# A fused windowed-attention and Fourier-mixing kernel in fp32: the probabilities of the first two batches turned by small products with the identity into tiles that hold two heads, and the first sines written to tiles that are not yet in use

## The chip, the cores and the metric

The kernel runs on one core of one Trainium2 chip. The metric is the device time in microseconds (us) of one launch; the kernel before took a median of 601.89 us in 3 runs (600.99 to 602.36). A core has five engines that are named here as the profile names them: PE (TensorE, matrix products; PEld is its weight load), DVE (VectorE), ACT (ScalarE), POOL (GpSimd) and SP (SyncE, which issues the loads and stores). Each engine takes its own instructions strictly in the order of the program, and semaphores order them between engines.

## The reference

Eight batches, eight heads, 576 positions, head size 64, with q, k and v in fp32 and the weights in 64-bit floats. Heads 0 to 3 see a window of 32 positions, heads 4 to 7 a window of 32 positions at every fourth one. The attention's result, heads side by side, is the x of a mixing layer of width 512.

```python
scores = np.where(masks, scale * q @ k.T, -1e9)
attn = exp(scores - scores.max(-1)); attn = attn / (attn.sum(-1) + 1e-9)
x = heads_side_by_side(attn @ v)                  # (8, 576, 512)
theta = x @ w_theta
zr, zi = x * np.cos(theta), x * np.sin(theta)
y = einsum('ts,bsd->btd', w_tok_r, zr) + einsum('ts,bsd->btd', w_tok_i, zi)
u = x + y
out = u + np.maximum(u @ w_ch, 0.0)
```

## The kernel before

**Tiling.** Heads go in four pairs. The dilated heads' positions are sorted on the host so that every head sees a plain window, and the 576 queries of a pair fall into 9 blocks of 64, each against its block of 64 keys and the one ahead. x, y, u and the output are held as four tiles of 128 features by 576 positions. Products that need fp32 precision run in three: a number is split into a high part in a shorter format (a cast) and a low part (the rest, a subtraction on POOL or DVE), and high by high, high by low and low by high are summed.

**Stages of a batch.** Names are those of tiles in the profile.
- *Attention, per pair.* 18 score products s (L426) of 64 moving columns; mask and row maximum on DVE (L401, into P and mx); exponentials on ACT (L452, nine of 128x64 a pair, with their sums sm; for batch 0 one, L441); sum and reciprocal on DVE (L455, L456); P times the reciprocal on POOL (L458). P has the queries on its partitions, so it is turned before the next product: into pt, the matrix that holds each block's transposed probabilities. From batch 1 on that is done by `turn` (L462 to L477), 8 stream transposes of 32x288 on DVE a pair (L474). For batch 0 it is `flip` (L494 to L515): 9 transposes a pair on PE against the identity idt (L509) in three groups of three, in three PSUM banks, and 12 copies of 64x96 a pair out of them, four on DVE (L487) and eight on ACT (L490). pt is four tiles of 128x9x64, one a head, so that two pairs alternate; the parts outside the window are zeroed once at the start. Then 18 products with v give o (L561), and ACT copies o to x (L525). From batch 1 on x is split in xh for the theta product (L537 ACT, L541 and L543 on DVE or POOL).
- *Trigonometry, per step of 128 positions* (five steps, in the order 4, 0, 1, 2, 3; step 4 has 64 positions). theta th (L606 for batch 0, L624 to L631 later); x transposed to positions on partitions, xn (L658); K is theta over 2 pi rounded (ACT, L680) and then its remainder (DVE, L682); g is its sine (L688); the absolute value and the cosine are taken in K's place (L637, L639); both are multiplied by xn on DVE (L694 for the sine, L644 for the cosine). `zsplit` (L577) splits each product: the high part zh is cast on DVE for batch 0 (L582) and on ACT later (L585), the low part zl is a subtraction on POOL (L587). The tiles K and g have two buffers each (tags f and g), so that a third step can begin only when the first one's zl is done. The zh and zl tiles have a tag for each of the nine (kt 0 to 3 cosines, 4 to 7 sines, 8 step 4).
- *Mixing.* y (L738): per tile of 128 features and half of the positions 27 products, three for each of the nine z; residual u = x + y on DVE (L716), its cast on ACT (L719) and low part on POOL (L721); then the channel product c (L767), 12 a tile, the final max and sum on DVE (L746), and the store.
- *Weights.* They come as 64-bit floats, and are turned into fp32 on DVE (L324, L334 or L329) and ACT (L326, L332), and split by ACT (L342) and POOL (L344). All of this lies before about 120 us.

**What sets the order.** For batch 0 and the part of batch 1's attention that runs beside it, tasks are generators that name an engine and a cost at each step, and the class `Order` (L56) plays them through: the engine that is free first takes the ready task of lowest rank (table RANK). The order that comes out is fixed in the program for every engine. A task can also wait for a named event (for instance ("P", 1, 2): P of batch 1, pair 2) or take one of several buffers. From batch 1's mixing on, loops set the order (`phase`), with batch n+1's attention inside batch n's products.

```python
        if b == 0:
            yield "DVE", dve2(DM)
            pin(nc.vector.tensor_copy(hi, z))
        else:
            yield "ACT", act(DM)
            pin(nc.scalar.copy(hi, z))
```

Of the kernel before, what the change touches and what calls it, by code (L numbers as in the profile page):

```python
# [34 lines left out]
STS = (4, 0, 1, 2, 3)  # L35
KORD = (0, 4, 1, 5, 2, 6, 3, 7, 8)
# [109 lines left out]
def build(ctx, tc, qT, kT, vw, wth, wtk, wch, masks, ident, outT):  # L146
# [315 lines left out]
    def turn(b, pr):  # L462

        yield None, "pts"
        yield None, ("P", b, pr)
        yield None, ("pv",) + divmod(b * NP + pr - 2, NP)
        P, rp = probs.pop((b, pr))
        o = 2 * (pr % 2)
        pmats[b, pr] = pts[o:o + 2]
        for i, (hh, e, o) in enumerate(strips()):  # L470
            if i % 2 == 0:
                yield "DVE", 940
            k0, p0 = QB * (2 * e + o), QB * (2 * e + hh)
            pin(nc.vector.transpose(pmats[b, pr][hh][k0:k0 + QB, :, QB * e:QB * e + QB],  # L474
                                    P[p0:p0 + QB, :, QB * o:QB * o + QB]))
        give("P", rp)
        signal(("pt", b, pr))  # L477

    def flip_evac(ps, rel, pr, m, key):
        for hh in range(2):  # L480
            for e in range(2):
                p0 = QB * (2 * e + hh)
                dst = pmats[0, pr][hh][BW * e:BW * e + BW, 3 * m:3 * m + 3, QB * e:QB * e + QB]
                src = ps[:, :, p0:p0 + QB]
                if m == 0:
                    yield "DVE", 170
                    pin(nc.vector.tensor_copy(dst, src))  # L487
                else:
                    yield "ACT", 174
                    pin(nc.scalar.copy(dst, src))  # L490
        give(*rel)
        signal(key)

    def flip(pr):  # L494
        yield None, ("P", 0, pr)
        if pr >= 1:
            yield None, ("fl", 0, pr - 1)
        if pr >= 2:
            yield None, ("pv", 0, pr - 2)
        yield None, "pts"  # L500
        o = 2 * (pr % 2)
        pmats[0, pr] = pts[o:o + 2]
        P, _ = probs.pop((0, pr))
        for m in range(3):
            ps, rel = yield from bank("mmt"[m], f"pT{pr}_{m}")
            ps = ps[:BW, :3 * 128].rearrange("p (a b) -> p a b", b=128)
            yield "PE", 330
            for n in range(3):
                pe(nc.tensor.transpose(ps[:, n], P[:, 3 * m + n], idt))  # L509
            go(flip_evac(ps, rel, pr, m, ("fe", pr, m)))  # L510
        signal(("fl", 0, pr))
        for m in range(3):
            yield None, ("fe", pr, m)
        give(f"xh{pr}", 0)
        signal(("pt", 0, pr))  # L515
# [31 lines left out]
    def pv(b, pr):  # L547
# [10 lines left out]
        for j in range(NJ):  # L558
            v = va[:, j] if j < VA else vb[:, j - VA]
            for hh in range(2):  # L560
                pe(nc.tensor.matmul(ps[64 * hh:64 * hh + 64, BW * j:BW * j + BW], v[:, 64 * hh:64 * hh + 64],  # L561
                                    pmats[b, pr][hh][:, j], start=True, stop=True))
# [14 lines left out]
    def zsplit(b, kt, z):  # L577
        hi = hp.tile([128, DM], F32R, tag=f"zh{kt}", name=f"zh{b}_{kt}")
        lo = hp.tile([128, DM], F32R, tag=f"zl{kt}", name=f"zl{b}_{kt}")
        if b == 0:  # L580
            yield "DVE", dve2(DM)
            pin(nc.vector.tensor_copy(hi, z))  # L582
        else:
            yield "ACT", act(DM)
            pin(nc.scalar.copy(hi, z))  # L585
        yield "POOL", pool(DM)
        pin(nc.gpsimd.tensor_tensor(lo, z, hi.bitcast(F32), op=ALU.subtract))  # L587
        zs[b, kt] = (hi, lo)
        signal(("z", b, kt))
# [45 lines left out]
    def cosine(b, st, f, z, kt, key):  # L635
# [10 lines left out]
        if kt is not None:  # L646
            yield None, ("px", b, st)
            give(*rx)
            yield from zsplit(b, kt, z)
# [12 lines left out]
    def trig(b, st):  # L662
# [5 lines left out]
        K = gp.tile([128, DM], I32, tag="f", name=f"K{b}_{st}")[:R]  # L668
        f = K.bitcast(F32)
        gt = gp.tile([128, DM], F32, tag="g", name=f"g{b}_{st}")  # L670
# [18 lines left out]
        if R == 128:  # L689
            go(cosine(b, st, f, f, st, ("cos", b, st)))  # L690
# [5 lines left out]
            yield from zsplit(b, 4 + st, g)  # L696
        else:
# [4 lines left out]
            yield from cosine(b, st, f, g, None, ("cos", b, st))  # L702
            give(*rx)
            yield from zsplit(b, 8, gt)
# [19 lines left out]
    def token(b, d, g):  # L724
# [6 lines left out]
        for kt in KORD:  # L731
# [5 lines left out]
            for l, r in ((zh, wh), (zh, wl), (zl, wh)):  # L737
                pe(nc.tensor.matmul(ps, l[:, cs], r, start=(n == 0), stop=(n == 3 * NK - 1)))  # L738
                n += 1
        go(residual(b, d, g, ps, rel), RANK["evacuate"])  # L740
# [193 lines left out]
```

## Time and profile before

| quantity | value |
|---|---|
| runs | 601.89, 600.99, 602.36 us, median 601.89 |
| profiled execution | 601.59 us, its span 599.8 us (1.8 us lie outside), mean granted clock 0.982 |
| first exponential of batch 1 on ACT | 65.75 us |
| first score product of batch 2, third pair | 147.20 us |

The page gives each engine's busy time and share of the span, and the span in 40 slices of 15 us with a digit for the busy tenths and for the TensorE clock that was granted. Other views of the same trace are used beside it: windows (busy time of each engine in each stretch), waits (an instruction that stood idle, its releaser, and how long), groups (all instructions of a line and shape, busy time, mean ns of one, idle time ahead), a timeline (start, length, instruction, with idle time in brackets), and the chain of work that ended last. A few records can be missing.

### The profile page before, as it was taken

To read this page: it belongs to the slowest core of one execution; us is meant where nothing else is said; L and a number is where in the kernel's file an instruction comes from. 1 tells how busy PE (TensorE), PEld (TensorE's weight loads), DVE (VectorE), ACT (ScalarE), POOL (GpSimd) and SP (SyncE) were. 2 spreads that over 40 slices of the span, in tenths; PEclk is the share of its full clock that TensorE was granted. 3 is DMA by queue.
4 is the path that set the end of the run, shared out by engine and by line. 5 is a ranking of instruction groups with operands and counts; after the bars stand their busy time and mean duration, and the time that the engine had idled before them with its cause. 6 is when DMAs were issued, how large, how long until landed. Compare 5 with 4: busy or idle time off the path is not lost.

```text
span 599.8 us, 14024 instructions
## 1 busy us (share of the span) xinstructions
PE 567.4 (95%) x5428; PEld 513.8 (86%) x5428; DVE 367.2 (61%) x1264; ACT 354.5 (59%) x959; POOL 222.5 (37%) x208
## 2 busy tenths in 40 slices
PE   4897599889999999999999999999999999999997
PEld 4644599779998899988998899988998899989997
DVE  3879898775566567656665657655764656444112
ACT  1796958767553974468564784359555685267010
POOL 2237846435142442316324252225323252315220
PEclk9998699999999999999999999999999999999999
DMA  8973347302541054401741035400642022001102
GB/s 322 396 278 99 121 163 246 136 0 87 196 139 61 1 186 148 149 1 40 240 142 61 0 142 180 151 11 17 228 141 97 1 81 97 2 1 42 37 1 80
DMA packets 26722, 67.82 MB, mean 113 GB/s; under 512 B 2848, under 2 KB 3104, under 8 KB 26656
## 3 DMA queue, kind: packets, MB, share of 16 engines
q1 hardware_dynamic: 26656, 66.92, 32.1%
q8 instruction: 43, 0.70, 0.5%
q14 instruction: 23, 0.19, 0.1%
HBM read 57.48 MB, written 9.44 MB: 112 GB/s over the span
## 4 chain that ended last, share of the span: by engine, by line
PE 42%; DVE 25%; ACT 21%; DMA 5%; issue 3%; POOL 3%; SPq 0%; ACTq 0%; POOLq 0%; DVEq 0%
PE y L738 21%; DVE pt L474 11%; PE c L767 9%; ACT P L452 7%; PE o L561 4%; PE th L624 3%; DVE P L401 3%; PE s L426 3%; ACT zh L585 2%; ACT K L639 2%; DVE K L644 2%; ACT g L688 2%; ACT K L637 2%; POOL P L458 2%; PE th L606 2%
## 5 line engine op out<-in xcount | busy, mean ns | idle before, releaser
L721 POOL TENSOR_TENSOR u<-x,u 128x288 fp32r<-128x288 f32 x64 | 54.2, 847 | 186.9 <-ACT u L719 171.5
L474 DVE STREAM_TRANSPOSE pt<-P 32x288 f32<-32x288 f32 x224 | 105.1, 469 | 23.5 <-POOL P L458 20.4
L767 PE MATMUL c<-u,late_wc 128*128 128x288 f32 x768 | 112.9, 299 | 2.2 <-DVE x L716 1.4
L767 PEld LDWEIGHTS c<-u,late_wc 128*128 128x128 f32 x768 | 107.2, 190 | 6.4 <-DVE x L746 2.0
L719 ACT CAST u<-x 128x288 fp32r<-128x288 f32 x64 | 27.4, 430 | 133.4 <-DVE x L716 133.4
L452 ACT ACTIVATE P<-P,mx 128x64 f32<-128x64 f32 x252 | 84.1, 336 | 17.6 <-DVE mx L446 17.4
L738 PE MATMUL y<-wtkh,zh 128*128 128x288 f32 x288 | 91.3, 317 | 3.0 <-DVE zh L582 3.0
L738 PE MATMUL y<-wtkh,zl 128*128 128x288 f32 x288 | 86.5, 300 | 0.9 <-POOL zl L587 0.9
L738 PE MATMUL y<-wtkl,zh 128*128 128x288 f32 x288 | 86.5, 300 | 0.0
L587 POOL TENSOR_TENSOR zl<-g,zh 128x512 fp32r<-128x512 f32 x40 | 52.1, 1302 | 77.4 <-ACT zh L585 64.4
L624 PE MATMUL th<-wthh,xh 128*128 128x512 f32 x224 | 75.9, 400 | 0.0
L716 DVE TENSOR_TENSOR x<-y,x 128x288 f32<-128x288 f32 x64 | 28.8, 451 | 66.7 <-PE y L738 66.4
L738 PE MATMUL y<-late_wt_b,zh 128*128 128x288 f32 x320 | 68.0, 296 | 0.0
L738 PEld LDWEIGHTS y<-wtkh,zh 128*128 128x128 f32 x288 | 55.6, 193 | 6.6 <-DVE zh L582 3.3
L738 PE MATMUL y<-late_wt_a,zh 128*128 128x288 f32 x256 | 57.1, 304 | 2.0 <-DVE x L716 2.0
L738 PEld LDWEIGHTS y<-wtkh,zl 128*128 128x128 f32 x288 | 55.6, 193 | 1.3 <-POOL zl L587 1.3
L738 PEld LDWEIGHTS y<-wtkl,zh 128*128 128x128 f32 x288 | 55.7, 193 | 0.8 <-POOL wtkl L344 0.5
L587 POOL TENSOR_TENSOR zl<-K,zh 128x512 fp32r<-128x512 f32 x32 | 41.9, 1309 | 36.5 <-ACT zh L585 35.1
L401 DVE CUSTOM_DVE_ANT_0 P<-s,msk 128x64 f32<-128x64 f32 x288 | 45.5, 220 | 15.1 <-PE s L426 8.3
L458 POOL TENSOR_TENSOR P<-P,sm 128x576 f32<-128x576 f32 x32 | 38.2, 1197 | 43.6 <-DVE sm L456 22.2
L738 PEld LDWEIGHTS y<-late_wt_b,zh 128*128 128x128 f32 x320 | 51.3, 188 | 0.5 <-POOL late_wt_b L344 0.2
L624 PEld LDWEIGHTS th<-wthh,xh 128*128 128x128 f32 x224 | 42.1, 188 | 8.1
(98 smaller groups left out, 1104.7 us busy)
## 6 DMA issues: line engine op xcount, KB each, us to landing
q<-in_qT_dram SPq DMA_DIRECT2D x32, 576.0 KB, 4.2
va<-in_vw_dram SPq DMA_DIRECT2D x30, 320.0 KB, 2.9
out_dram<-x SPq DMA_DIRECT2D x32, 288.0 KB, 2.1
k<-in_kT_dram SPq DMA_DIRECT2D x28, 304.0 KB, 4.5
vb<-in_vw_dram SPq DMA_DIRECT2D x29, 256.0 KB, 3.1
st_wtk<-in_wtk_dram SPq DMA_DIRECT2D x8, 576.0 KB, 7.8
st_wth<-in_wth_dram SPq DMA_DIRECT2D x4, 512.0 KB, 8.5
st_wch<-in_wch_dram SPq DMA_DIRECT2D x4, 512.0 KB, 3.7
```

The lines of the kernel that those rows point to most:

```text
L401: pin(nc.vector.tensor_tensor_reduce(out=P[:, n], in0=ps[:, n - g0], in1=msk[:, mask_of(pr, n)], op0=ALU.add, op1=ALU.max, scale=1.0, scal ...
L452: table(nc.scalar.activation(P[:, n], P[:, n], AF.Exp, bias=mx[:, n:n + 1], scale=SCALE, accum_out=sm[:, n:n + 1]))
L458: pin(nc.gpsimd.tensor_tensor(P, P, sm.unsqueeze(2).to_broadcast([128, NJ, BW]), op=ALU.mult))
L474: pin(nc.vector.transpose(pmats[b, pr][hh][k0:k0 + QB, :, QB * e:QB * e + QB], P[p0:p0 + QB, :, QB * o:QB * o + QB]))
L561: pe(nc.tensor.matmul(ps[64 * hh:64 * hh + 64, BW * j:BW * j + BW], v[:, 64 * hh:64 * hh + 64], pmats[b, pr][hh][:, j], start=True, stop=T ...
L587: pin(nc.gpsimd.tensor_tensor(lo, z, hi.bitcast(F32), op=ALU.subtract))
L624: pe(nc.tensor.matmul(pt, l, r, start=(n == 0), stop=(n == 3 * NC - 1)))
L716: pin(nc.vector.tensor_tensor(x[:, ts], ps, x[:, ts], op=ALU.add))
L719: pin(nc.scalar.copy(uh[b, d][:, ts], x[:, ts]))
L721: pin(nc.gpsimd.tensor_tensor(ul[b, d][:, ts], x[:, ts], uh[b, d][:, ts].bitcast(F32), op=ALU.subtract))
L738: pe(nc.tensor.matmul(ps, l[:, cs], r, start=(n == 0), stop=(n == 3 * NK - 1)))
L767: pe(nc.tensor.matmul(ps, l[:, cs], r[:, ts], start=(n == 0), stop=(n == 3 * NC - 1)))
```

## The change

- The tile pt is two tiles of 128x9x2x64, both heads of a pair in one, instead of four; `pv` (L561) and `turn` take their parts from there.
- `flip` takes the batch as an argument and is used for batches 0 and 1; `turn` stays for batches 2 to 7. A pair is turned by 18 products of 64x64 with a 64x64 corner of the identity (L512 of the changed kernel), in two PSUM banks of five and four blocks, and taken out by four copies: the first halves of the two groups by DVE (L487, 64x320 and 64x256 elements), the second halves by ACT (L490).
- The steps 4, 0 and 1 of batch 0's trigonometry have K and g in tiles that the later z of steps 2 and 3 would use (FG0: zl2, zl6, zl3, zl7, zh3, zh7), so only steps 2 and 3 take the two buffers of f and g. The planner takes and gives these buffers by name, and `zsplit` gives them back.
- The cosines' high parts of batch 0 (kt 0 to 3) are cast on ACT, the sines' on DVE as before.
- `zsplit` of batch 1 waits in the planner for the token products of batch 0.

```diff
+FG0 = {4: ("zl2", "zl6"), 0: ("zl3", "zl7"), 1: ("zh3", "zh7")}
...
-        for n in range(4):
-            t = cp.tile([128, NJ, 2 * QB], F32, name=f"pt{n}")
-            yield "POOL", 520
+        for n in range(2):
+            t = cp.tile([128, NJ, 2, 2 * QB], F32, name=f"pt{n}")
+            yield "POOL", 1040
...
-            pin(nc.vector.transpose(pmats[b, pr][hh][k0:k0 + QB, :, QB * e:QB * e + QB],
+            pin(nc.vector.transpose(pmats[b, pr][k0:k0 + QB, :, hh, QB * e:QB * e + QB],
                                     P[p0:p0 + QB, :, QB * o:QB * o + QB]))
...
+    def flip_evac(b, ps, rel, pr, g0, g1, key):
+        for e in range(2):
+            es, qs = slice(BW * e, BW * e + BW), slice(QB * e, QB * e + QB)
+            n = (g1 - g0) * BW
+            if e == 0:
+                yield "DVE", dve(n)
+                pin(nc.vector.tensor_copy(pmats[b, pr][es, g0:g1, :, qs], ps[es]))
+            else:
+                yield "ACT", act(n)
+                pin(nc.scalar.copy(pmats[b, pr][es, g0:g1, :, qs], ps[es]))
...
+        gs = (0, 5), (5, NJ)
+        for i, (g0, g1) in enumerate(gs):
+            ps, rel = yield from bank("mt"[i] if b == 0 else "xt"[i], f"pT{b}_{pr}_{g0}")
+            ps = ps[:, :(g1 - g0) * BW].rearrange("p (a h b) -> p a h b", h=2, b=QB)
+            yield "PE", 70 * (g1 - g0)
+            for n in range(g0, g1):
+                for e in range(2):
+                    es = slice(BW * e, BW * e + BW)
+                    pe(nc.tensor.matmul(ps[es, n - g0].rearrange("p a b -> p (a b)"), P[es, n], idt[es, es],
+                                        start=True, stop=True))
+            go(flip_evac(b, ps, rel, pr, g0, g1, ("fe", b, pr, g0)))
...
-                                    pmats[b, pr][hh][:, j], start=True, stop=True))
+                                    pmats[b, pr][:, j, hh], start=True, stop=True))
...
+    def zsplit(b, kt, z, rel):
+        if b == 1:
+            for d in range(NC):
+                yield None, ("tk", 0, d, 1)
...
-        if b == 0:
+        if b == 0 and kt >= NC:
             yield "DVE", dve2(DM)
             pin(nc.vector.tensor_copy(hi, z))
...
+        if b == 0 and st in FG0:
+            K, gt = (hp.tile([128, DM], F32R, tag=t, name=f"{n}{b}_{st}").bitcast(F32) for t, n in zip(FG0[st], "Kg"))
...
+        else:
+            rf, rg = ("f", (yield from take("f", 2))), ("g", (yield from take("g", 2)))
...
-        go(flip(p), RANK["flip"] + p * RANK["pair"])
+        go(flip(0, p), RANK["flip"] + p * RANK["pair"])
...
-        go(turn(1, p), RANK["scores1"] + p * RANK["pair"])
+        go(flip(1, p), RANK["scores1"] + p * RANK["pair"])
```

Since the planner works with other tasks, the order of every engine ahead of batch 1's last channel products is new. From the score product at 147.20 us on, all five engines have the same order as before. In the rows below a name is followed by batch or pair and step, and by a number that only tells tiles apart.

The first place is the trigonometry of batch 0. DVE before, at the first cosine products; zh is the high part, K the cosine's tile, g the sine's:

```order
L694 TENSOR_TENSOR g_1_615<-xn_1_616,g_1_615 128x512
L324 TENSOR_SCALAR st_wtk_1_369<-st_wtk_1_369 128x576
L582 CAST zh_5_654<-g_1_615 128x512
L694 TENSOR_TENSOR g_2_627<-xn_2_632,g_2_627 128x512
L644 TENSOR_TENSOR K_1_614<-xn_1_616,K_1_614 128x512
L582 CAST zh_6_671<-g_2_627 128x512
L582 CAST zh_1_677<-K_1_614 128x512
```

ACT now, at the same place:

```order
L700 ACTIVATE K_1_592<-th_1_411 128x512
L335 ACTIVATE st_wtk_3_279<-st_wtk_3_279 128x576
L329 ACTIVATE st_wtk_4_270<-st_wtk_4_270 128x288
L595 CAST zh_0_608<-K_0_530 128x512
L708 ACTIVATE g_1_593<-K_1_592 128x512
L649 ACTIVATE K_1_592<-K_1_592 128x512
L345 CAST wtkh_623<-st_wtk_3_279 128x576
L651 ACTIVATE K_1_592<-K_1_592,halfpi 128x512
L700 ACTIVATE K_2_638<-th_2_472 128x512
L345 CAST wtkh_643<-st_wtk_4_270 128x288
L595 CAST zh_1_656<-K_1_592 128x512
```

The casts zh_0 and zh_1 of cosines have moved from DVE to ACT, between its sines and weights.

The second place is DVE at the turn of batch 1's first two pairs (P_0, P_1), beside the residuals x_0 and x_1 of batch 0. Before:

```order
L716 TENSOR_TENSOR x_0_300<-y_0_0_658,x_0_300 128x288
L474 STREAM_TRANSPOSE pt_103<-P_0_539 32x9x32 x2
L334 SCALAR_TENSOR_TENSOR st_wtk_2_419<-st_wtk_2_419 128x576
L474 STREAM_TRANSPOSE pt_103<-P_0_539 32x9x32 x2
L474 STREAM_TRANSPOSE pt_107<-P_1_731 32x9x32 x2
L474 STREAM_TRANSPOSE pt_105<-P_0_539 32x9x32 x2
```

Now:

```order
L736 TENSOR_TENSOR x_0_268<-y_0_0_632,x_0_268 128x288
L458 TENSOR_SCALAR sm_1_718<-sm_1_718 128x9
L459 RECIPROCAL sm_1_718<-sm_1_718 128x9
L487 COPY pt_103<-pT_0_0_834 64x10x32
L337 SCALAR_TENSOR_TENSOR st_wtk_1_349<-st_wtk_1_349 128x576
L487 COPY pt_103<-pT_0_5_856 64x8x32
L487 COPY pt_105<-pT_1_0_877 64x10x32
```

DVE copies from the PSUM banks pT where it turned, and the copies stand behind x_0.

The third place is PE, where pair 2's scores s_2, the o product of pair 0 and the flips stand between the products y. Before:

```order
L426 MATMUL s_2_0_922<-k_2_736,q_2_735 64x64 x10
L738 MATMUL y_2_0_890<-wtkh_578,zh_7_758 128x288
L738 MATMUL y_2_0_890<-wtkl_579,zh_7_758 128x288
L738 MATMUL y_2_0_890<-wtkh_578,zl_7_759 128x288
L426 MATMUL s_2_5_942<-k_2_736,q_2_735 64x64 x8
L738 MATMUL y_2_0_890<-wtkh_643,zh_8_609 128x288
L738 MATMUL y_2_0_890<-wtkl_644,zh_8_609 128x288
L738 MATMUL y_2_0_890<-wtkh_643,zl_8_610 128x288
L561 MATMUL o_0_918<-pt_103,va_0_439 64x64
```

Now, one y later, the flip of that pair (s_2 itself stands at the beginning of y_2, and the eight z steps behind it, o_0 and s_3 lie ahead of these rows):

```order
L758 MATMUL y_3_0_1089<-wtkh_509,zh_0_608 128x288
L758 MATMUL y_3_0_1089<-wtkl_510,zh_0_608 128x288
L758 MATMUL y_3_0_1089<-wtkh_509,zl_0_609 128x288
L512 MATMUL pT_2_0_1076<-idt,P_2_894 64x64 x10
L758 MATMUL y_3_0_1089<-wtkh_537,zh_4_572 128x288
L758 MATMUL y_3_0_1089<-wtkl_538,zh_4_572 128x288
L758 MATMUL y_3_0_1089<-wtkh_537,zl_4_573 128x288
L512 MATMUL pT_2_5_1112<-idt,P_2_894 64x64 x8
```

The scores have moved ahead by most of a y, and PE has the flip as a new thing that waits for P.

More of the change, by code (lines that the diff above doesn't have):

```diff
@@ L491, in flip_evac, with flip @@
         give(*rel)
         signal(key)
-    def flip(pr):
-        yield None, ("P", 0, pr)
+    def flip(b, pr):
+        yield None, ("P", b, pr)
         if pr >= 1:
-            yield None, ("fl", 0, pr - 1)
-        if pr >= 2:
-            yield None, ("pv", 0, pr - 2)
+            yield None, ("fl", b, pr - 1)
+        if b or pr >= 2:
+            yield None, ("pv",) + divmod(b * NP + pr - 2, NP)
         yield None, "pts"
[L501 to L515, printed above, removed]
+        pmats[b, pr] = pts[pr % 2]
+        P, rp = probs.pop((b, pr))
+        gs = (0, 5), (5, NJ)
[9 more added lines that the diff above has]
+            go(flip_evac(b, ps, rel, pr, g0, g1, ("fe", b, pr, g0)))
+        signal(("fl", b, pr))
+        for g0, _ in gs:
+            yield None, ("fe", b, pr, g0)
+        if b == 0:
+            give(f"xh{pr}", 0)
+        else:
+            give("P", rp)
+        signal(("pt", b, pr))
@@ L648, in cosine @@
             give(*rx)
-            yield from zsplit(b, kt, z)
+            yield from zsplit(b, kt, z, rel)
+        elif rel:
+            give(*rel)
     pxs = {}
```

36 lines of the change are left out of this document (14 added, 22 removed).

## The prediction, made before the change was run

> **What bounds the kernel now.** I read the page's engine shares first, then the granted clock, then busy time by stage, then what TensorE (PE) waited for in the weak stages.
>
> ```profile
> span 599.8 us, 14024 instructions
> PE 567.4 (95%) x5428; PEld 513.8 (86%) x5428; DVE 367.2 (61%) x1264; ACT 354.5 (59%) x959; POOL 222.5 (37%) x208
> PEclk9998699999999999999999999999999999999999
> ```
>
> PE is busy in 95% of the span, so over the whole program it is the bound; the granted clock dips in one slice alone, the fifth. The stages tell more. The columns are the stretch, its length, busy time of PE, PEld, DVE, ACT and POOL with instruction counts, granted PE clock, DMA share and GB/s.
>
> ```profile
> 48.00:71.00 23.00, 13.46 (x91) 8.64 (x90) 21.26 (x53) 17.87 (x52) 18.07 (x14) 0.75 0.43 144
> 71.00:77.00 6.00, 6.00 (x27) 6.00 (x28) 4.99 (x10) 5.71 (x15) 5.58 (x5) 0.52 0.00 0
> 77.00:112.00 35.00, 34.75 (x454) 31.61 (x453) 31.04 (x131) 23.46 (x81) 16.99 (x16) 1.00 0.68 232
> 112.00:147.00 35.00, 30.77 (x180) 27.08 (x178) 23.05 (x45) 26.02 (x55) 15.90 (x14) 0.95 0.05 19
> 147.00:599.80 452.80, 445.20 (x4298) 417.38 (x4296) 253.59 (x883) 250.66 (x692) 151.88 (x146) 1.00 0.27 90
> ```
>
> From 147 us on PE is 98% busy at full clock. There the instructions of batches 2 to 7 stand in the same order on every engine in both kernels, so this stretch does not change: the question is only when PE comes to 147. Ahead of it, 48 to 71 us is the hole: PE works 13.5 of 23 us at 0.75 of its clock, and then 6 us at 0.52. These are its waits from 48 to 71 us (total, times, longest):
>
> ```profile
> PE y L738 <- DVE zh L582: 3.0, 1, 3.0
> ...
> PE s L426 <- DVE mx L401: 1.7, 1, 1.7
> PE y L738 <- POOL zl L587: 0.9, 1, 0.9
> ```
>
> PE waits for the trigonometry of batch 0, whose products z enter y split into a high (zh) and a low part (zl). The timeline (start, length) shows the end of that hole on ACT, POOL and PE.
>
> ```profile
> 65.75 0.35 ACT L452 ACTIVATE P<-P,mx 128x64 f32<-128x64 f32 x1
> ...
> 69.02 1.71 POOL L587 TENSOR_TENSOR zl<-K,zh 128x512 fp32r<-128x512 f32 x1 [0.36 <-DVE zh L582]
> ...
> 70.78 0.61 PE L738 MATMUL y<-wtkh,zl 128*128 128x288 f32 x1 [0.94 <-POOL zl L587]
> ```
>
> At 65.75 ACT is through with the sines and begins the exponentials of batch 1. The low part of the last cosine (step 3) is done on POOL at 69.02 + 1.71 = 70.73 and releases PE at 70.78. From there PE runs nearly without gaps.
>
> **A. The first sines, in unused tiles, and the cosine casts on ACT.** K and g have two buffers each, so the third step of batch 0 waits until the first step's low part is done; ACT shows that from 36 to 72 us. The two rows behind are the stretches from ACT's first K (39.47) to its exponentials, and from POOL's first low part (46.35) to its last; then the casts.
>
> ```profile
> ACT K L680 <- POOL zl L587: 5.1, 2, 4.0
> 39.47:65.75 26.28, 20.64 (x132) 12.31 (x132) 23.61 (x64) 21.15 (x35) 17.50 (x14) 0.88 0.36 122
> 46.35:70.73 24.38, 14.89 (x96) 9.24 (x94) 22.91 (x56) 19.24 (x54) 19.45 (x15) 0.77 0.40 135
> L582 DVE CAST zh<-K 128x512 fp32r<-128x512 f32 x4 | 5.1, 1272 | 0.0
> L585 ACT CAST zh<-K 128x512 fp32r<-128x512 f32 x4 | 2.5, 622 | 1.0 <-DVE K L644 1.0
> ```
>
> The change gives three of the five steps tiles of their own, so both waits go, and moves four cosine casts from DVE (1272 ns each, 5.1 us) to ACT (622 ns each, as batch 1 has them there).
> - ACT: in 26.3 us it works 21.15, and the 5.1 are those waits. It starts about 1 us earlier (39.47 to 38.5), since it makes 2 copies a pair for batch 0 instead of 8. Added: four casts, 2.5; three exponentials of 0.33 to 0.35 that now stand ahead of the last cast, 1.0. Removed: the unpacking of the second half of a late weight, which now stands behind, 1.5. So 38.5 + 21.2 + 2.5 + 1.0 - 1.5 = 61.7 against 65.75: ACT is no longer the late one.
> - POOL: of the 24.4 us it works 19.45 and idles 4.9, and its instructions stay the same. If it starts 1 us earlier and never idles it ends at 45.3 + 19.5 = 64.8, that is -5.9; if half of the idle time stays, at about 68.3, -2.4.
>
> I take 1 us of idle time, 65.8, so **-4.9** (bounds -5.9 and -2.4), nearer the full gain since both things it waited for, casts on DVE and ACT's list, come earlier. The 1 us is for the cast of the last cosine, which still has to come before POOL.
>
> **B. Batch 1 turned on PE.** The four pairs of batch 1 are no longer turned by 32 of DVE's transposes but by 18 products of 64x64 with the identity a pair, between PE's other work. No such product is in the trace; the nearest in shape, with the same number of moving columns, are the score products.
>
> ```profile
> 82.23 0.69 PE L426 MATMUL s<-k,q 128*64 128x64 f32 x16
> ...
> 102.88 0.80 PE L426 MATMUL s<-k,q 128*64 128x64 f32 x20
> 147.20 1.20 PE s L426 x36
> 148.40 3.77 PE y L738 x27
> 152.17 1.20 PE o L561 x36
> L474 DVE STREAM_TRANSPOSE pt<-P 32x288 f32<-32x288 f32 x48 | 22.5, 469 | 3.8 <-POOL P L458 3.0
> L487 DVE COPY pt<-pT 64x96 f32<-64x96 f32 x16 | 3.9, 245 | 1.0 <-PE pT L509 0.7
> ```
>
> The profile counts two records a product, so x20 and x16 are 10 and 8 products: 0.80 + 0.69 = 1.49 us a pair in two pieces, and 1.20 where 36 records run unbroken. Four pairs cost **+6.0** (bounds 4.8, unbroken, and 6.4 if every piece is as slow as 0.80). DVE loses 32 x 469 ns = 15.0 us and gets 8 copies of 64x320 or 64x256 at about 0.45 (an estimate from 245 ns for 64x96), 3.6; ACT gets as many, also 3.6. DVE works 31.0 of the 35 us from 77 to 112, so it is eased there; ACT at 23.5 has room. Batch 0's own flips lie before 48 us: 9 transposes a pair of twice the columns give way to 18 products, and 12 copies to 4. That is the same count of columns, so PE is the same there, and the copies' gain is the 1 us in A; if that 1 us is not there, A is -3.9. In later batches one tile holds both heads, so DVE writes with twice the stride: the same count of elements, no cost taken.
>
> By the Trainium skill (TensorE: Matmul & The Clock Gate, "Terms"), plain FP32 streams four passes while a transposing product is four times faster. Taken as 64 columns x 4 at its 2.4 GHz, 18 products would be an estimated 1.92 us a pair, 7.7 in all, and the sum 1.7 higher. The score row, plain FP32 too with 1.20 a pair, speaks against that price here.
>
> **C. Losses of before that go.** PE idles 0.25 us from 77 to 112 and 4.23 from 112 to 147; the waits behind most of it:
>
> ```profile
> PE th L628 <- ACT xh L537: 1.6, 1, 1.6
> PE c L767 <- DVE x L716: 1.4, 1, 1.4
> ```
>
> The half clock costs 6.0 x (1 - 0.52) = 2.9 us from 71 to 77, and 30.77 x 0.05 = 1.5 from 112 to 147. In sum 4.5 + 2.9 + 1.5 = **-8.9**, all given back at first, since the order of PE from 71 to 147 is new.
>
> **D. New losses.** Each has its rows.
>
> ```profile
> 59.70:63.10 3.40, 1.77 (x37) 1.33 (x32) 3.40 (x5) 3.40 (x6) 3.04 (x4) 0.99 0.58 212
> 63.00:64.00 1.00, 0.11 (x2) 0.14 (x4) 1.00 (x10) 1.00 (x3) 1.00 (x2) 0.53 0.57 217
> 76.00:77.00 1.00, 1.00 (x7) 1.00 (x7) 0.96 (x3) 0.91 (x2) 1.00 (x1) 0.65 0.00 0
> 86.26 0.33 ACT L452 ACTIVATE P<-P,mx 128x64 f32<-128x64 f32 x1
> ...
> 90.27 0.42 DVE L455 TENSOR_SCALAR sm<-sm 128x9 f32<-128x9 f32 x1 [1.26 <-ACT P L452]
> ...
> 91.11 1.15 POOL L458 TENSOR_TENSOR P<-P,sm 128x576 f32<-128x576 f32 x1 [0.45 <-DVE sm L456]
> ```
>
> - Clock: it fell to half at 63.1, behind 3.4 us in which PE worked 1.77, and came back at 76.5 after some 6 us of full work, 4 x 3.4 us later. PE stays thin until 65.8, so full clock should return at 63.1 + 2 x 3.4, near 70: (70 - 65.8) / 2 = 2.1.
> - Flips that wait: PE's queue is in program order, and a flip stands between other products, so a late P stops all of them. The last three rows follow pair 2 of batch 1 before: scores done at 82.23 + 0.69 = 82.9, exponentials from 86.26, sums at 90.27, P done at 92.26, 9.3 us in all. Of that, 3.3 lie ahead of the exponentials, while DVE ends a turn and unpacks weights; without turns I take 1.0. The exponentials with what lies between took 4.0; I take 4.3, for the o evacuation that now stands there. The rest stays 2.0. So 7.3 against 6.8 us of PE work (eight z steps of y_2 and one of y_3 at 3.77 / 9 = 0.42 are 3.8, o_0 1.2, s_3 1.5, and 0.3 of hand-overs): 0.5 late. Pair 3's last exponentials stand behind ACT's copies of pair 2: copies 0.8, three exponentials 1.0, the rest 2.0, in sum 3.8, against 5.2 of PE work (o_1 1.2, two score pieces 1.5, six z steps 2.5); I take 0.5 for what stands ahead of it on POOL.
> - The channel product now stands closer behind y_3: c_0 waits for the last residual and the splits of u, 1.7 (the 1.4 of before and 0.3). The x split of pair 3 for theta, 1.6 before, is read later: 0.5.
>
> In sum 2.1 + 0.5 + 0.5 + 1.7 + 0.5 = **+5.3**.
>
> The Trainium skill (TensorE: Matmul & The Clock Gate, Part 1) has the clock fall only after a whole idle window. The row at 59.7, 52% busy ahead of the fall, shows less idleness than that is enough here. By the rule the short new waits cost no clock; by the row they can.
>
> **The sum.** -4.9 + 6.0 - 8.9 + 5.3 = -2.5. The profiled execution took 601.59 us (599.8 of span and 1.8 around it), the median of the three runs is 601.89, so 601.6 - 2.5 = **599.1**.
>
> **Rivals.**
> - *The flips stop PE (slower).* Pair 2 still needs its 9.3 us where PE has 6.8 of work, 2.5; pair 3 comes late in turn by 0.9 (3.8 and two more products of 1.15 on POOL against 5.2); each wait has a half-clock window of 3.4 us behind it, 1.7. That is 6.8 in place of the 1.0 of D, about +5.7: 604.8. It decides once P comes more than some 1.5 us late. For it: ACT and POOL, which the chain also passes, keep their late weights, and ACT gets the copies. Against: DVE, which it passes three times, is eased by 11 us.
> - *Everything early (faster still).* POOL never idles (-5.9) and PE, packed with flips and scores, is busy enough from 60 us on to keep its clock: A gains 1.0 more, D loses 2.1, and the late waits shrink by 1.2, so 594.8. Against: PE still has 9.5 us of hole between 48 and 71.
> - *ACT takes the place of the tiles (no change).* The four casts stand in ACT's list between sines and weights; if each comes late, POOL keeps half of its idle time, A is -2.4 and the sum 0: 601.5. For it: ACT works 17.9 of 23 us there already.
>
> **How the numbers follow.** Forecast 0.42, everything early 0.18, ACT 0.14, flips that stop PE 0.26. A change of 0.2% (1.2 us) is about what can be told from none. So faster by more than that 0.60, within it 0.14, slower 0.26. The range: at the low end the faster rival with 1.3 for the price of the flips (4.8 for 6.0), 593.5; at the high end the slower rival, 604.5; the forecast's own range, A between its bounds and each wait doubled or gone, is 596 to 602.
>
> **What would show it.** A: the last low part of batch 0 ends near 65.8 on POOL, and ACT has no wait for a K tile. B: 72 flip products in batch 1 at about 1.5 us a pair. C and D: the first score product of batch 2's third pair, before at 147.2, comes at 144.7, with less idle time and half clock between. Wrong would be: PE waiting over 1.5 us for P or for a copy in front of a pT, or the half clock lasting as long as before; or a change behind 147.

## The result, and the profile after

The changed kernel is slower: a median of 606.55 us in 5 runs (604.43 to 607.45) against 601.89, a ratio of 1.008 with an interval of 1.0064 to 1.0095. Run once more beside 17 runs of the kernel before, its ratio was 1.0087 (1.0072 to 1.0103). The forecast was 599.1, with 604.5 as the upper end.

The profiled execution took 604.43 us with a span of 602.7, 2.9 more than before; it was the fastest of its five. A second profile of the same kernel (first experiment) has a span of 604.1. It is behind by 1.3 us before 20 us: 0.35 of that is a load, and the rest comes because PE had its full clock later (its first flip took 2.19 us there, for 1.26). It differs little from there. A difference of 1 us between two single profiles therefore says nothing, and verdicts below go by the medians.

The page of the changed kernel, first its engines and clock:

```profile
PE 571.1 (95%) x5680; PEld 517.8 (86%) x5680; DVE 355.8 (59%) x1228; ACT 357.0 (59%) x947; POOL 222.2 (37%) x206
...
PEclk9998699899999999999999999999999999999999
```

PE has 3.7 us more work, DVE 11.4 less, ACT 2.5 more, and one more slice, the eighth, has lost clock (the fourth and the fifth read as before). The windows of the stages (stretch, length, busy time of PE, PEld, DVE, ACT, POOL, granted clock, DMA share, GB/s), as before:

```profile
48.00:71.00 23.00, 17.06 (x114) 12.13 (x114) 19.46 (x52) 20.63 (x62) 19.78 (x16) 0.70 0.36 118
71.00:77.00 6.00, 6.00 (x93) 5.08 (x89) 3.98 (x9) 5.62 (x11) 4.63 (x4) 1.00 0.00 0
77.00:112.00 35.00, 30.27 (x466) 26.48 (x467) 25.87 (x117) 30.01 (x106) 16.91 (x15) 0.99 0.62 216
112.00:147.00 35.00, 34.36 (x208) 31.07 (x208) 18.28 (x34) 23.26 (x37) 14.46 (x14) 0.96 0.06 21
```

The hole before 71 us is smaller (PE works 17.1 of 23 us for 13.5). But from 77 to 112 us PE works 30.3 of 35 us where it worked 34.75, and ACT has taken DVE's place: 30.0 for 23.5, while DVE went from 31.0 to 25.9. The waits of PE from the last low part of batch 0 to the first score product of batch 2's third pair name what is late:

```profile
PE o L568 <- ACT x L532: 3.8, 1, 3.8
PE y L758 <- POOL zl L597: 1.7, 1, 1.7
PE pT L512 <- POOL P L461: 1.0, 2, 0.6
PE xn L672 <- DVE g L656: 0.4, 1, 0.4
```

The first row is new. The o product of batch 1's last pair waits for ACT to copy the o of the pair before out of the one PSUM buffer that both use. The timeline shows PE there, and ACT (its exponentials, nine of them in this stretch, are left out):

```profile
106.25 0.29 PE L758 MATMUL y<-late_wt_b,zl 128*128 128x288 f32 x1
110.31 0.80 PE L568 MATMUL o<-pt,va 128*64 128x64 f32 x20 [3.77 <-ACT x L532]
```

```profile
103.37 0.68 ACT L345 CAST late_wc<-st_wch 128x512 fp32r<-128x512 f32 x1 [1.79 <-DVE st_wch L337]
103.96 0.67 ACT L329 ACTIVATE st_wch<-st_wch 128x512 f32<-128x512 f32 x1
...
105.53 0.66 ACT L335 ACTIVATE st_wch<-st_wch 128x512 uint32<-128x512 uint32 x1
...
107.08 0.41 ACT L739 CAST u<-x 128x288 fp32r<-128x288 f32 x1
...
108.41 0.63 ACT L345 CAST late_wc<-st_wch 128x512 fp32r<-128x512 f32 x1
109.06 1.19 ACT L532 COPY x<-o 128x576 f32<-128x576 f32 x1
```

The o of pair 2 was complete at 102.0. ACT began its copy at 109.06, since unpackings and casts of a late weight and the exponentials of the next batch stand ahead of it in ACT's order. ACT was not working all of these 7.1 us: for the first 1.4 it stood idle ahead of the cast at 103.37, which waited for DVE's unpacking. The clock follows, in three windows of 3.4 us:

```profile
104.49:107.90 3.41, 2.05 (x16) 1.81 (x14) 3.15 (x7) 3.41 (x18) 1.28 (x2) 1.00 0.41 150
107.90:111.31 3.41, 1.00 (x34) 1.00 (x36) 1.60 (x5) 3.00 (x7) 2.65 (x3) 1.00 0.00 0
111.31:114.73 3.42, 3.42 (x23) 3.30 (x20) 3.32 (x8) 2.23 (x3) 1.14 (x3) 0.50 0.51 173
```

PE works 29% of the window from 107.9, and gets half clock in the next one, where it works without a gap: 1.7 us on top of the 3.8.

Two stretches make the balance. The first ends where the low part of batch 0's last cosine lets PE go on (70.78 us before); the second runs from there to the first score product of batch 2's third pair (147.13 before in the timeline; the chain has it at 147.20). The windows of the second stretch and of the rest, before and then after:

```profile
70.78:147.13 76.35, 71.86 (x656) 64.91 (x656) 59.08 (x184) 55.54 (x151) 38.82 (x34) 0.94 0.33 115
147.13:599.80 452.67, 445.07 (x4297) 417.38 (x4296) 253.59 (x883) 250.53 (x692) 151.75 (x146) 1.00 0.27 90
```

```profile
67.40:149.94 82.54, 77.17 (x801) 68.84 (x801) 50.97 (x161) 62.93 (x168) 40.08 (x35) 0.96 0.31 107
149.94:602.70 452.76, 445.33 (x4297) 417.52 (x4296) 253.60 (x883) 249.48 (x691) 150.47 (x144) 1.00 0.27 90
```

The rest is the same (452.67 and 452.76). PE is let go 3.4 us earlier, and the second stretch is 6.2 us longer: PE's work at full clock is 77.17 x 0.96 = 74.1 for 71.86 x 0.94 = 67.5, 6.6 more, and idle time and half clock together 8.4 for 8.8. So -3.4 + 6.6 - 0.4 = +2.8, which is the shift of the score product from 147.13 to 149.94. The clock is rounded to 0.01, so up to 0.7 us can move between the last two terms.

### The profile page after: what moved, and what is told of

Its sections match the earlier page's. It is cut to its first block, busy times and chain, and to the rows that moved or that the text cites. A ratio compares the mean times of both kernels' runs of the same rounds, so it can differ in the third digit from the quotient of the medians.

```text
span 602.7 us, 14503 instructions
## 1 busy us (share of the span) xinstructions
PE 571.1 (95%) x5680; PEld 517.8 (86%) x5680; DVE 355.8 (59%) x1228; ACT 357.0 (59%) x947; POOL 222.2 (37%) x206
## 4 chain that ended last, share of the span: by engine, by line
PE 37%; ACT 26%; DVE 25%; DMA 5%; issue 4%; POOL 3%; ACTq 0%; DVEq 0%; SPq 0%
PE y L758 19%; DVE pt L476 10%; PE c L788 8%; ACT P L455 8%; DVE P L404 3%; ACT zh L595 3%; PE th L636 3%; ACT K L651 3%; PE o L568 3%; PE s L429 3%; ACT g L708 3%; ACT K L649 2%; DVE K L656 2%; DVE xh L550 2%; DMA q<-in_qT_dram 2%
## 5 line engine op out<-in xcount | busy, mean ns | idle before, releaser
L788 PE MATMUL c<-u,late_wc 128*128 128x288 f32 x768 | 110.4, 296 | 0.7 <-DVE x L767 0.2
L788 PEld LDWEIGHTS c<-u,late_wc 128*128 128x128 f32 x768 | 105.8, 188 | 4.5 <-DVE x L767 1.9
L476 DVE STREAM_TRANSPOSE pt<-P 32x288 f32<-32x288 f32 x192 | 90.1, 469 | 20.0 <-POOL P L461 17.5
```

Of the source, the lines that this page charges most:

```text
L476: pin(nc.vector.transpose(pmats[b, pr][k0:k0 + QB, :, hh, QB * e:QB * e + QB], P[p0:p0 + QB, :, QB * o:QB * o + QB]))
L788: pe(nc.tensor.matmul(ps, l[:, cs], r[:, ts], start=(n == 0), stop=(n == 3 * NC - 1)))
```

## The experiments

All runs, with the ratio to the kernel before on the same chip. "Released" is the start of the y product that reads the low part of step 3's cosine, "scores" that of the first score product of batch 2's third pair, both in the run's one profile; "stretch" is their difference.

| run | median us | ratio (95%) | released | scores | stretch |
|---|---|---|---|---|---|
| before | 601.89 | | 70.78 | 147.13 | 76.35 |
| after | 606.55 | 1.008 (1.0064 to 1.0095) | 67.40 | 149.94 | 82.54 |
| after again | 607.0 | 1.0087 (1.0072 to 1.0103) | 68.66 | 151.45 | 82.79 |
| o copy first | 604.05 | 1.0042 (1.0028 to 1.0056) | 67.74 | 148.54 | 80.80 |
| batch 1 on DVE | 601.48 | 0.9997 (0.9987 to 1.0008) | 67.62 | 147.77 | 80.15 |
| sines in f, g | 607.82 | 1.0102 (1.0087 to 1.0116) | 72.32 | 153.31 | 80.99 |
| flips twice | 607.82 | 1.0105 (1.0087 to 1.0123) | 67.03 | 155.54 | 88.51 |
| casts on DVE | 603.79 | 1.0041 (1.0027 to 1.0055) | 67.80 | 148.53 | 80.73 |
| batch 0's part, buffers planned | 610.93 | 1.0147 (1.0128 to 1.0166) | 71.52 | 154.25 | 82.73 |
| two pairs flipped | 605.37 | 1.0059 (1.0042 to 1.0076) | 67.51 | 150.82 | 83.31 |
| copies on DVE | 605.44 | 1.0068 (1.0052 to 1.0085) | 68.04 | 151.03 | 82.99 |
| casts, copies on DVE, o copy first | 603.15 | 1.0028 (1.0017 to 1.0038) | 66.83 | 147.68 | 80.85 |
| the same, flips twice | 605.64 | 1.0073 (1.0054 to 1.0093) | 67.74 | 150.86 | 83.12 |
| batch 0's flips alone | 604.30 | 1.0054 (1.0034 to 1.0074) | 66.83 | 149.23 | 82.40 |
| sines alone | 600.61 | 0.9984 (0.9973 to 0.9995) | 68.91 | 146.45 | 77.54 |
| sines and casts | 599.90 | 0.9977 (0.9961 to 0.9994) | 68.77 | 146.34 | 77.57 |

An edit that changes what a task costs or takes also changes the planner's order behind it. Only the two runs with flips issued twice keep the order of their base.

**The changed kernel again**, no edit.

> The changed kernel once more, nothing edited, for a second profile. Theory 1 (a queue on ACT): the o product of pair 3 of batch 1 again waits 3 to 4 us for ACT's copy of pair 2's o, with a half-clock stretch of some 3.4 us behind it; median 605.5 to 607.5. Rival (the wait is an accident of the profiled run, and the loss lies elsewhere): the wait is under 1 us in this profile and the span still 2 to 5 us longer than that of the kernel before.

The wait for ACT's copy is there again, 3.8 us, with half clock from 113.2 to 116.6. It belongs to the program's order.

**The o copy first.**

```diff
-        go(x_evac(b, pr, ps, ("v", n), ("xe", b, pr)))
+        go(x_evac(b, pr, ps, ("v", n), ("xe", b, pr)), 0 if (b, pr) == (1, 2) else None)
```

> One edit in the changed kernel: ACT's copy of pair 2's o product (batch 1) gets the first rank, so it stands ahead of two unpackings, six exponentials and a cast in ACT's order. Theory 1: the wait of 3.8 us and the half clock of 1.7 us behind it go, 606.5 - 5.5 = 601. Rival 2 (PE is bound by the sum of what ACT, POOL and DVE have to do in this stage, so that the wait moves to the next product): 605 or more, with a wait of 2 us or more at another line between 95 and 130 us.

The time lay between the two: 3 us less. The wait of 3.8 and its half clock are gone, but the waits of the same stretch are now

```profile
PE y L758 <- POOL zl L597: 1.7, 1, 1.7
PE xn L672 <- DVE g L656: 1.2, 1, 1.2
PE th L636 <- DVE g L697: 1.0, 1, 1.0
PE pT L512 <- POOL P L461: 0.9, 2, 0.6
PE o L568 <- DMA vb<-in_vw_dram: 0.8, 1, 0.8
```

Of the 5.5 us hoped for 3 came, and the rest went to shorter waits: the copy was the longest late thing, not the only one.

**Batch 1 on DVE.**

```diff
-        go(flip(1, p), RANK["scores1"] + p * RANK["pair"])
+        go(turn(1, p), RANK["scores1"] + p * RANK["pair"])
```

> The changed kernel with batch 1 turned by DVE's stream transposes again; the two-head tiles, batch 0's flips, the first sines and the cosine casts stay as changed. Theory 1: the flips' 6.0 us of PE time go, and with ACT's eight copies the queue ahead of the o copy: 606.5 - 6.0 - 3 to 5 = 595.5 to 597.5. Rival 2 (DVE becomes late in place of PE): the gain is eaten by waits for pt, 601 or more.

Without the flips of batch 1 the kernel is 5.5 us faster (607.0 to 601.48). What remains is level with the kernel before, not 4 to 6 us under it: the rival's 601. PE's release is 3.2 us earlier and the stretch behind is 3.8 longer, although PE's work there is that of before (72.66 us busy at 0.94). Its waits:

```profile
PE c L788 <- DVE x L767: 2.2, 1, 2.2
PE y L758 <- POOL zl L597: 1.7, 1, 1.7
PE o L568 <- DMA vb<-in_vw_dram: 1.7, 1, 1.7
PE y L758 <- DVE x L736: 0.9, 1, 0.9
PE c L788 <- DVE x L736: 0.8, 1, 0.8
PE s L429 <- issue: 0.8, 1, 0.8
PE o L568 <- DVE pt L476: 0.8, 1, 0.8
```

DVE, which still turns batch 1, and a load are late now.

**Sines in f and g.**

```diff
-FG0 = {4: ("zl2", "zl6"), 0: ("zl3", "zl7"), 1: ("zh3", "zh7")}
+FG0 = {}
```

> The changed kernel with no sines in unused tiles: steps 4, 0 and 1 take the two f and g buffers as before, all else as changed. Theory 1: ACT waits some 5 us for the buffers again, the last low part of batch 0 comes about 3.4 us later (67.4 to 70.8), and the time is 609 to 611. Rival 3 (the tiles gain nothing, the casts on ACT take their place): 606 to 607, with the last low part still near 67 to 68.

The release came at 72.32, 3.7 to 4.9 us after that of the two profiles of the changed kernel, more than expected. The time rose by 0.8 us only, since the stretch behind is 1.6 to 1.8 us shorter. The o copy's wait does not occur in this order, and there is less half clock (mean clock 0.990 in all four runs, for 0.980 to 0.986 in the six of the changed kernel beside it). So the run shows that the release comes later without the tiles, but not what an earlier one is worth with all else equal.

**Each flip of batch 1 twice.**

```diff
-                    pe(nc.tensor.matmul(ps[es, n - g0].rearrange("p a b -> p (a b)"), P[es, n], idt[es, es],
-                                        start=True, stop=True))
+                    for _ in range(1 + b):
+                        pe(nc.tensor.matmul(ps[es, n - g0].rearrange("p a b -> p (a b)"), P[es, n], idt[es, es],
+                                            start=True, stop=True))
```

> The changed kernel with each of batch 1's 72 flip products issued twice into the same place; the order is the same otherwise. Theory 1 (a flip's PE time lies bare, 1.48 us a pair): four times 1.48 more, less at most 1 us where waits for P or for ACT's copy take it up: 607.0 + 5 to 6 = 612 to 613. Rival (the flips lie in time that PE has anyway, and the loss is waits alone): 609 or less.

The rival's number: 607.82, 0.8 us more (1.1 by the ratios, with intervals that overlap). How much was added is read from the pieces of pair 1 in the timeline:

```profile
76.48 1.43 PE L513 MATMUL pT<-idt,P 64*64 64x64 f32 x40
...
78.44 1.20 PE L513 MATMUL pT<-idt,P 64*64 64x64 f32 x32
```

With 0.80 and 0.68 for one issue each, a second one adds 0.63 and 0.52, so 1.15 a pair and 4.6 in all, less than the 6.0 that was expected.

The small difference does not show that the flips lie in time that PE has anyway. The stretch of this run's profile:

```profile
67.03:155.54 88.51, 84.34 (x945) 75.94 (x945) 51.89 (x161) 62.93 (x168) 40.07 (x35) 0.93 0.30 100
```

PE's work at full clock is 84.34 x 0.93 = 78.4 us for the changed kernel's 74.1, 4.3 more; its idle time is 4.2 for 5.4 (the o copy's wait 2.9 for 3.8), and half clock costs 5.9 for 3.1. So all but 1.2 us of the added work lay bare in this execution (it made the stretch longer one for one), and more half clock came on top. It took 609.95 us with a mean clock of 0.980. The five others took 607.07 to 608.03 at 0.991, and the changed kernel's eleven had 0.980 to 0.989, most of them 0.986. A difference of 0.005 in 605 us is 3 us of clock, nearly as much as is missing. Whether the rest of the 4.6 us fell into idle time in those five, or lay bare and was paid back by the clock, stays open.

**Casts on DVE.**

```diff
-        if b == 0 and kt >= NC:
+        if b == 0:
```

> The changed kernel with the cosines' high parts of batch 0 cast on DVE as before (1272 ns each for 622 on ACT); the rest as changed. If moving the casts is what brings the last low part forward: it comes 2 to 3 us later than at 67.4 to 68.7, and the time is 608 to 610. Rival (ACT is the late engine there, and the casts on it cost what they save): the same within 1 us, 606 to 607.5.

Neither: the release stays at 67.80, as the rival had it, and the time falls by 3.2 us. The casts on ACT brought PE nothing there. On ACT they took 2.4 us, on DVE 3.1 in this run (5.1 in the kernel before). Why the time falls is not shown: the o copy's wait is still 3.0 us and PE's idle time in the stretch 5.2 for 5.4, but the half-clock window behind that wait is missing.

**Batch 0's part of the change, first try.** `turn(1, p)`, `FG0 = {}` and the casts on DVE, in the changed kernel.

> Only the two-head tiles and batch 0's small flips of the change: batch 1 turned on DVE, first sines in f and g, cosines cast on DVE, all as before. If the parts add up: between 601.5 (all of the change but batch 1's flips) and 603, so that sines and casts gain 0 to 1.5. If the small flips are a gain or a loss of their own: under 600, or over 604.

It came out at 610.93, outside every expectation. PE waits 6.6 us there for a cosine product, in one piece that ends at 61.5 us. This run is not the part alone: the planner now takes buffers f and g by name, which the kernel before did not tell it, and so plans another order. The run of batch 0's flips alone, below, separates this.

**Two pairs flipped.** `flip` for pairs 0 and 1 of batch 1, `turn` for 2 and 3.

> The changed kernel with pairs 0 and 1 of batch 1 flipped on PE and pairs 2 and 3 turned on DVE. Theory 1 (each flipped pair costs its 1.48 us of PE, and the o copy's wait goes since ACT has four copies less): 601.5 + 3.0 = 604.5 at most, and less by what DVE's turns of pairs 0 and 1 made PE wait, so 600 to 603. Rival (no gain from easing DVE): 604 to 605.

605.37, the rival's side by a little. The o copy's wait is gone, but y waits 3.2 us for DVE's residual and theta 2.0 for ACT's split of x.

**Copies on DVE.**

```diff
-            if e == 0:
+            if e == 0 or b == 1:
                 yield "DVE", dve(n)
```

> The changed kernel with all 16 copies of batch 1's flips on DVE, none on ACT. Theory 2, formed after the flips issued twice (ACT, not PE, sets the pace from 77 to 112 us, where it is busy 30.0 of 35 us against 23.5 in the kernel before): ACT loses 8 copies of 0.37 to 0.42, 3.2 us, and the o product's wait for ACT's copy shrinks from 3.8 to 2 or less: 603 to 605. Rival (the flips' time on PE decides): 606 to 607, as the products stay.

1.6 us less (1.1 by the ratios, with intervals that overlap), just outside the expected 603 to 605. The o copy's wait is gone, but the stretch is no shorter (82.99): a P comes 2.5 us late in front of a flip, and theta waits 2.3 for DVE.

**Casts and copies on DVE, o copy first**, the three edits together.

> The changed kernel with the cosine casts and all copies of batch 1's flips on DVE, and pair 2's o copy first in ACT's order; sines in unused tiles and all flips as changed. Theory 2: what ACT got is taken off it, 5.7 us, and the last wait on it goes: 607.0 - 3.2 (casts) - 3.0 (o copy first) + 1 for what both saved = 600 to 602. Rival (PE's 6.0 us of flips stay bare): 604 or more.

603.15, between the two, and 3.9 us under the changed kernel. ACT works 25.35 us from 77 to 112 and PE 32.69:

```profile
77.00:112.00 35.00, 32.69 (x494) 28.80 (x490) 27.57 (x119) 25.35 (x96) 17.10 (x15) 1.00 0.65 220
```

**The same with each flip twice.**

> The kernel of the run with casts, copies and the o copy taken off ACT's queue (603.15), with each of batch 1's 72 flip products issued twice. Theory 2 (PE is the bound again once ACT is relieved): 4 to 6 us more, 607 to 609. Rival (PE has room for the flips in any case): 605 or less.

2.5 us more (2.7 by the ratios), between the two expectations, for 4.6 us of PE work. The stretches of the two profiles, once and twice, have the same clock:

```profile
66.83:147.68 80.85, 75.66 (x801) 67.61 (x801) 56.82 (x171) 58.36 (x165) 43.18 (x36) 0.98 0.34 117
67.74:150.86 83.12, 80.12 (x945) 72.09 (x945) 55.40 (x171) 58.40 (x165) 42.59 (x36) 0.98 0.32 113
```

PE is busy 4.5 us more and idle 3.0 us for 5.2, so the stretch grows by 2.3: here about half of what was added lay bare, and half went into waits.

**Sines alone.** The kernel before with FG0 and what belongs to it (buffers f and g taken by the planner, batch 1's split waiting for batch 0's token products).

> The kernel before with one part of the change: the sines of steps 4, 0 and 1 of batch 0 in unused tiles. The four-tile pt, its flips for batch 0, the turns of batch 1 on DVE and the cosine casts on DVE stay as before. If the part is a gain by itself: the last low part of batch 0 comes 3 to 4 us before 70.78, and the time is 598 to 600. If what comes earlier there is given back behind it, by waits for DVE and the loads: 601 to 603, with the stretch from that low part to the score product at 147.1 longer by 3 to 4 us.

600.61, a little short of the first expectation, and faster than before with an interval that ends at 0.9995. The release comes 1.9 us earlier, and the stretch behind is 1.2 longer. Of the 1.9, 1.2 lie ahead of ACT's first K (38.23 for 39.47), which is no more than two profiles of one kernel differ by (38.55 and 39.82 for the changed one).

**Batch 0's flips alone.** The two-head tiles and small flips for batch 0; trigonometry, splits and turns of batch 1 as before.

> The kernel before with the two-head tiles and batch 0's small flips only; unlike the earlier run of that part, the trigonometry is word for word that of before, so the planner does not take buffers f and g. If the small flips themselves cost the 9 us of that run: 609 or more. If the planner's buffers did: 600 to 603, with the order of batch 0's trigonometry as before.

604.30, between the two expectations: the flips of batch 0, with the order that the planner makes for them, cost some 3 us (ratio 1.0054). The other 6.6 us of the first try came with what that run has besides: the planner takes the buffers f and g by name without tiles for the first sines, and batch 1's splits wait for batch 0's token products. The release comes at 66.83, 4.0 us early, and everything is lost again behind it, by waits of the stretch:

```profile
PE c L775 <- DVE x L754: 3.0, 1, 3.0
PE o L568 <- DVE pt L476: 2.2, 2, 1.7
PE y L745 <- DVE x L723: 2.0, 2, 1.8
PE y L745 <- POOL late_wt_b L347: 1.9, 1, 1.9
```

**Sines and casts.** The sines alone, and the cosine casts of batch 0 on ACT.

> The kernel before with the sines in unused tiles and the cosine casts on ACT; flips and turns as before. Theory 2 (ACT pays 2.5 us for the casts and z comes no earlier by them): 600.6 + 0 to 2.5, so 600.6 to 603. If DVE's 5.1 us less counts more: 598 to 600.

599.90 against 600.61: inside the second expectation, but not to be told from the sines alone. It is the fastest version here, 0.23% under the kernel before (0.9977, 0.9961 to 0.9994).

The parts in a chain, each with the planner's order that belongs to it: before 1; with sines 0.9984; with casts 0.9977; with batch 0's flips and the two-head tiles 0.9997; with batch 1's flips 1.0087. In us of 602 that is -1.0, -0.4, +1.2 and +5.4. The steps hold for this chain only: batch 0's flips alone cost 3 us, not 1.2, and the casts, which cost nothing here, cost 3.2 in the changed kernel.

## Why the prediction was wrong, point by point

- **What bounds, and that the rest stays.** Right: batches 2 to 7 took 452.67 and 452.76 us.
- **A, the release of PE.** The direction was right, the size was not: -3.4 in the profile (-2.1 in the second), for -4.9. The 1 us of it for an earlier start is not shown: ACT's first K, 39.47 before, came at 38.55 and 39.82 in the two profiles, and at 38.23 with the sines alone, which keep the old copies. From that K to the release it took 31.3 us before and 28.8 in both profiles, so 2.5 for the other 3.9. ACT does not wait for a K tile any more, but between its first K and its first exponential, at 63.16 rather than 61.7, it waited 1.1 us for a weight that DVE unpacks and 1.2 for DVE's cosine products. The cast of step 3's cosine stands behind three exponentials, at 64.17, and POOL took 1.89 of a theta weight's split before the low part at 66.02. Of the two reasons given, the tiles count in this kernel (32.9 us from K to release without them, though sines alone gain 0.6), and the casts do not (28.3 with them back on DVE). Batch 0's flips alone, with neither, bring 28.1: the new order did as much there.
- **B, the price of a flip.** This term held. The rows were the right ones: 0.80 for ten products and 0.68 for eight, as forecast, and 0.46 and 0.41 for DVE's copies, forecast as 0.45. The Trainium skill's four passes for plain FP32 (FP8 and Floating Point Precision, "TensorE Precision Notes"; the prediction names "Terms" of TensorE: Matmul & The Clock Gate, where the factor of four of the transposing mode stands), from which an estimate of 1.92 a pair came, do not fit: a pair took 1.48. And PE's work grew by as much. In the stretch, counted as busy time less half of what lay in half-clock windows, it is 67.4 to 68.2 us in the six profiles with batch 1 turned on DVE, 70.1 with two pairs flipped, 73.8 to 74.8 in the seven with four pairs, and 78.1 and 78.4 with each flip issued twice.
- **C, the losses of before.** In the changed kernel they went, as forecast: none of the waits that it lists is left. In size it was right as well: 8.8 in the stretch, or 8.9 with the half-clock windows counted one by one, as below. That a new order of PE has no reason to lose as much is not so in general: with PE's old work but batch 0's new flips, idle time and half clock in the stretch come to 12.7 us with batch 1 on DVE and to 14.3 with batch 0's flips alone, for 8.9 before. What PE gains at the front of the stretch, DVE's turns, the late weights and the loads have not gained, so PE waits for them further on.
- **D, the new losses.** This is the step that failed: 8.4 us of idle time and half clock came in the place of C's, for the 5.3 forecast. The waits for P were 0.58 and 0.39, for 0.5 each. The half clock behind the release ended at 70.35, so 1.5 us for 2.1. c_0 and theta did not wait at all, for 1.7 and 0.5, and xn waited 0.4. What was missing is the largest one, put at nothing: the o product of pair 3, 3.8 and a half-clock window of 1.7. The prediction asked which instructions on PE wait for P, and had put ACT's relief and burden down as sums (ACT "has room", 23.5 of 35 us); it did not follow ACT's order from the end of o_2 to its copy. C and D together were to bring -3.6 and brought -0.4 in the profiled execution.
- **The rivals.** The slower rival's 604.8 was the nearest number (the range ended 0.3 below it, at 604.5), by another place: P came late by 1.0 in sum, not 3.4, and the wait was behind the flips. ACT did take over as the late engine, as the third rival had it, but from 77 to 112 us rather than before 71.

The sum with what was measured in place of the forecast is -3.4 + 6.6 - 8.8 + 8.4 = +2.8, for -4.9 + 6.0 - 8.9 + 5.3 = -2.5: D is off by 3.1, A by 1.5, B by 0.6.

What the runs show is that batch 1's four flips add about 6.5 us to PE's work in the stretch, that with them idle time and half clock stay at 6.0 to 9.0 us, for 8.9 before, and that without them the time is 5.5 us lower. With one copy moved ahead in ACT's order the time is 3 us lower. That ACT's load as a whole is what the rest hangs on is not shown: with all copies of batch 1's flips on DVE, ACT was busy 58.6 us in the stretch for 62.9, and the stretch was no shorter; with the casts on DVE it was busy 62.6, and the time fell by 3.2. Each edit also brought a new order. What the flips would cost in an order made by hand for them was not tried.

## What to carry to other kernels

Where work is taken off one engine and given to others, follow the order of the receiving engine from the moment a single buffer is ready to be emptied to the instruction that empties it; ACT's 23.5 of 35 us looked like room, and with the change a copy that PE needed stood there for 7.1 us. A gain at the front of a stretch can be lost behind it, where other engines have not gained. And before a price is put on the path, do that work twice: it is a small edit that leaves the order alone. Read work, idle time and half clock of the two traces beside it, since the time alone also holds what the clock gave or took.

## What the runs showed of the hardware

The clock comes in windows of about 3.4 us, and a half-empty window was often enough to lose it. In the kernel before:

```profile
49.41:52.82 3.41, 1.38 (x6) 0.88 (x7) 3.06 (x5) 0.87 (x2) 2.51 (x2) 1.00 0.73 220
59.65:63.06 3.41, 1.82 (x39) 1.38 (x33) 3.41 (x4) 3.41 (x6) 3.05 (x4) 1.00 0.56 206
114.26:117.67 3.41, 1.70 (x10) 1.32 (x11) 2.83 (x6) 3.14 (x15) 3.32 (x4) 1.00 0.02 5
121.09:124.50 3.41, 2.50 (x16) 2.37 (x17) 3.30 (x7) 2.35 (x3) 0.81 (x1) 1.00 0.00 0
```

PE was busy 40%, 53% and 50% of the first three, and had half clock in the window behind each; behind the fourth, 73%, it kept its clock. In the changed kernel 60% (104.49 to 107.90) kept it, and 57% (53.29 to 56.70) and 29% lost it. The share alone does not decide: in the second profile of the changed kernel a window of about 50% kept it (1.6 to 1.8 us from 106.2 or 106.4, as its edges are set), and with batch 0's flips alone one of 48% (from 77.17). Over the sixteen traces, from 20 to 150 us, no window under 45% kept it and none of 60% or more lost it. The Trainium skill (TensorE: Matmul & The Clock Gate, Part 1) speaks of at least one idle window of about 3.4 us; the length agrees, and for the rows above "idle" has to be read as "about half idle".

How many such windows an execution has is not fixed by the program. The run with flips issued twice had a mean clock of 0.980 in its profiled execution and 0.991 in the other five, and took about 2 us more in the first. A single profile can thus carry windows that the median does not have.
